# An attention and MLP kernel: left rows in quarters of the array, left values inside the last block, left queries with the second half, and a written-out order

## The chip, the cores and the metric

The kernel runs on one core of a Trainium2 chip. A core has five engines that work side by side and each take their instructions in order: PE (the matrix engine, with PEld for its weight loads), DVE (VectorE), ACT (ScalarE), POOL (GpSimd) and SP (SyncE, which here only issues DMA transfers). The metric is device time in microseconds (us) of one execution, as the median of several runs; lower is better.

## The reference

Four batches of eight heads, 576 positions, head size 64. Rotary attention is followed by an MLP with a piecewise activation:

```python
scores = scale * np.matmul(q_rot, k_rot.transpose(0, 1, 3, 2))
scores = scores - np.max(scores, axis=-1, keepdims=True)
attn = np.exp(scores)
attn = attn / (np.sum(attn, axis=-1, keepdims=True) + 1e-09)
attn_out = np.matmul(attn, v)
x = attn_out.transpose(0, 2, 1, 3).reshape(B * S, H * D)      # 2304 x 512
h = x @ w_in                                                  # 512 x 2048
g = np.where(h >= 1, h, np.where(h <= -1, 0.0, (h + 1) ** 2 / 4.0))
return g @ w_out                                              # 2048 x 512
```

The data is drawn so large that one fp16 value is not enough. Every operand of a product is therefore kept as a sum of two fp16 numbers, and each product is three products (`TERMS`: high by high, high by low, low by high).

## The kernel before, in words

**Rows.** A batch has 576 query rows: four tiles of 128 (the main rows) and 64 left rows. Work goes in eight blocks, two for each batch: tiles 0 and 1, then tiles 2 and 3 (the batch's last block). The heads go in four pairs `j`.

**Scores and softmax.** One item is a tile and a pair of heads (`scores`, L582): 12 matmuls, in which the two heads use the upper and the lower 64 rows of the array and write `psS[0]` and `psS[1]`; three products of 512 columns and three of 64 columns for each head. The softmax of an item (`softmax_item`) is, for each head, a maximum on DVE (`mx`, L556), an exponential on ACT (L558), the high half of the normalised row on ACT (L566) and its low half on DVE (`phl`, L568). SP then issues a transposing DMA from `phl` into `pT` (L300).

**Values.** For a block and a pair of heads `pv_group` runs 28 matmuls (L611), 14 for each head, of 256 columns, the two heads side by side in the left and the right 64 columns of the array. After two pairs `x_out` moves 512 columns of `psV` to `xT` (ACT L626, DVE L629).

**The left rows** have a path of their own, after the last block of each batch (`attention_left`). `prep_left` loads, turns and splits their queries into `qL`, a tile with the two heads of a pair on the diagonal and zeros elsewhere. For each pair one full-width group of six matmuls (`scores_left`, L594) gives 64 rows of both heads in one tile `psS[z]`, a softmax over one such tile follows, one transposing DMA of half the size, and 28 matmuls of 64 columns (`pv_left`, L611). One `x_out` of 256 columns for each batch writes `xL`.

**The MLP** takes each block in 8 steps. A step is two groups of 12 matmuls of 256 columns into `psH` (L692), the activation (ACT L699, L711; DVE L702, L709, L713, the last of which writes the low half of `g`), and two groups of six matmuls of 512 columns into `psO` (L722). The left rows of two batches together make one more MLP of 4 steps with groups of 128 columns. So there are 72 steps in all.

**The weights** come as 64-bit floats. `prep_w` turns each of 16 chunks into two fp16 halves: three passes on DVE (L506, L508, L510) over a staging buffer, then work on ACT and on PE (L535, L536) or DVE (L527).

**The order.** Every step is entered into a `Plan` with its engine, an estimated cost and the keys it reads and writes. `Plan.order()` simulates the engines with these costs, takes at each point the step with the lowest rank, where the rank is a due time plus the numbers of the table `SLACK`, and returns one list. The steps are written into the program in the order of this list, so it sets the queue of each engine.

## Time and profile before

| | |
|---|---|
| median of 3 runs | 636.88 us |
| lowest and highest run | 633.86 and 639.57 us |
| span of the profiled execution, first to last instruction | 632.0 us |
| PE, DVE and ACT busy in that span | 559.8, 511.2 and 441.0 us |

The profile is of one execution. Its span leaves out what lies around the instructions, and of that execution only the span is known; it stands 4.88 us under the median of the runs. Busy times come from this one execution; durations of instructions that follow each other closely overlap a little, so that a chain of start times is a better measure of a group than the sum of its instructions.

### The profile page before, as it was taken

The page shows a single profiled execution, that of the slowest core. Times are in us where ns is not written, and L with a number is a line of the kernel's source. Part 1 is how long each engine was busy: PE and PEld are TensorE (multiplying, and loading weights), DVE is VectorE, ACT ScalarE, POOL GpSimd, SP SyncE. Part 2 cuts the span into 40 slices and gives each one's busy share as a digit, 9 for nine tenths or more (in the row PEclk, how much of TensorE's full clock was granted, in tenths as well). Part 3 has the DMA queues.
Part 4 walks back from the last instruction along what each step waited for, and adds up shares of the span by engine and source line. Part 5 has one row for each costly group of instructions (what it writes and reads, how often), then busy time and mean ns, then how long its engine had stood idle before and what let it go on. Part 6 is the DMA issues. An engine that isn't in the chain of part 4 may idle for free.

```text
span 632.0 us, 12652 instructions
## 1 busy us (share of the span) xinstructions
PE 559.8 (89%) x5078; PEld 358.6 (57%) x5078; DVE 511.2 (81%) x839; ACT 441.0 (70%) x881; POOL 7.5 (1%) x18
## 2 busy tenths in 40 slices
PE   1346678799997999999998999999999999999995
PEld 1112234566654666666665676676666676666663
DVE  5998999999999999998897889889877874333422
ACT  3647898978999799984878798877787663232221
POOL 0000100000000000000000000000000000000000
PEclk9997879999998999999999999999999999999999
DMA  8997988695699858876377765856666553000000
GB/s 265 372 305 261 258 231 161 133 233 132 142 260 203 195 99 188 205 164 161 92 163 129 124 127 109 136 94 115 113 131 129 85 99 77 1 8 27 1 34 18
DMA packets 188011, 91.33 MB, mean 145 GB/s; under 512 B 170160, under 2 KB 178608, under 8 KB 185904
## 3 DMA queue, kind: packets, MB, share of 16 engines
q1 hardware_dynamic: 186224, 77.94, 56.0%
q0 software_dynamic: 1728, 12.58, 5.6%
q8 instruction: 40, 0.66, 0.4%
q14 instruction: 19, 0.16, 0.1%
HBM read 40.96 MB, written 4.72 MB: 72 GB/s over the span
## 4 chain that ended last, share of the span: by engine, by line
PE 56%; DVE 22%; DMA 12%; ACT 6%; issue 3%; SPq 0%; ACTq 0%
PE psO L722 21%; PE psH L692 21%; PE psV L611 7%; PE psS L582 5%; DMA pT<-phl 5%; DVE phl L568 4%; DVE mx L556 3%; DMA rk<-in_km_dram 3%; DMA vM<-vS 2%; ACT p L558 2%; DVE g L713 1%; ACT phl L566 1%; DMA rv<-in_vm_dram 1%; DVE r L709 1%; DVE xT L508 1%
## 5 line engine op out<-in xcount | busy, mean ns | idle before, releaser
L722 PE MATMUL psO<-w,g 128*128 128x512 f16 x864 | 211.7, 380 | 1.9 <-ACT g L711 0.9
L692 PEld LDWEIGHTS <-w 128*128 128x128 f16 x1920 | 170.9, 98 | 44.4 <-issue 5.2
L692 PE MATMUL psH<-xT,w 128*128 128x256 f16 x1536 | 187.7, 273 | 3.2 <-ACT a L699 3.2
L558 ACT ACTIVATE p<-psS,mx 128x576 f32<-128x576 f32 x144 | 105.3, 733 | 26.1 <-DVE mx L556 20.1
L722 PEld LDWEIGHTS <-g 128*128 128x128 f16 x864 | 79.3, 98 | 75.2 <-DVE g L713 2.5
L568 DVE SCALAR_TENSOR_TENSOR phl<-p,sums,phl 128x576 f16<-128x576 f32 x144 | 113.4, 812 | 9.6 <-ACT phl L566 9.6
L566 ACT ACTIVATE phl<-p,sums 128x576 f16<-128x576 f32 x144 | 105.0, 765 | 17.5 <-DVE sums L563 15.2
L556 DVE TENSOR_REDUCE mx<-psS 128x1 f32<-128x576 f32 x144 | 104.3, 750 | 6.9 <-PE psS L582 6.2
L582 PE MATMUL psS<-kT,qT 64*128 64x512 f16 (+1 forms) x768 | 64.5, 295 | 22.6 <-ACT p L558 15.3
L711 ACT ACTIVATE g<-r 128x512 f16<-128x512 f32 x72 | 44.9, 624 | 47.5 <-DVE r L709 29.2
L699 ACT ACTIVATE a<-psH 128x512 f32<-128x512 f32 x72 | 42.4, 590 | 49.3 <-PE psH L692 48.7
L713 DVE SCALAR_TENSOR_TENSOR g<-r,g 128x512 f16<-128x512 f32 x72 | 49.5, 688 | 26.8 <-ACT g L711 26.7
L582 PEld LDWEIGHTS <-qT 64*128 64x128 f16 x768 | 31.2, 97 | 68.5 <-issue 47.9
L702 DVE SCALAR_TENSOR_TENSOR r<-a 128x512 f32<-128x512 f32 x48 | 33.1, 689 | 45.6 <-ACT a L699 45.2
L611 PE MATMUL psV<-pT,vS 128*64 128x256 f16 (+1 forms) x768 | 50.1, 253 | 3.8 <-DMA pT<-phl 3.5
L709 DVE SCALAR_TENSOR_TENSOR r<-a,r 128x512 f32<-128x512 f32 x72 | 49.6, 689 | 0.9
L611 PEld LDWEIGHTS <-vS 128*64 128x64 f16 x768 | 33.3, 112 | 18.5 <-issue 14.7
L611 PE MATMUL psV<-pT,vM 128*64 128x256 f16 (+1 forms) x480 | 29.2, 253 | 3.3 <-DMA vM<-vS 3.3
L558 ACT ACTIVATION_READ_ACCUMULATOR p<-psS,mx 128x1 f32 x144 | 28.1, 195 | 0.0
L692 PE MATMUL psH<-xL,w 128*128 128x128 f16 x384 | 25.5, 219 | 0.0
L611 PEld LDWEIGHTS <-vM 128*64 128x64 f16 x480 | 22.0, 113 | 4.1 <-DMA vM<-vS 3.8
L535 PE MATMUL psO<-xT,xL 128*128 128x512 f32 x20 | 15.4, 864 | 9.8 <-DVE xT L510 5.6
(98 smaller groups left out, 467.5 us busy)
## 6 DMA issues: line engine op xcount, KB each, us to landing
w<-in_w_in_dram POOLq DMA_DIRECT2D x5, 1024.0 KB, 6.9
rv<-in_vm_dram SPq DMA_DIRECT2D x8, 512.0 KB, 5.7
w<-in_w_out_dram POOLq DMA_DIRECT2D x4, 1024.0 KB, 7.3
out_dram<-o SPq DMA_DIRECT2D x16, 256.0 KB, 2.4
rq<-in_qm_dram SPq DMA_DIRECT2D x7, 512.0 KB, 7.2
dup<-in_qm_dram SPq DMA_DIRECT2D x7, 512.0 KB, 3.9
dup<-in_km_dram SPq DMA_DIRECT2D x6, 576.0 KB, 5.3
rk<-in_km_dram SPq DMA_DIRECT2D x6, 576.0 KB, 6.8
```

Of the source, the lines that this page charges most:

```text
L556: plan.add("dve", dve_cost(S, psum=True), at, lambda m=m, src=src: nc.vector.tensor_reduce(out=m, in_=src, op=ALU.max, axis=AX.X, negate=T ...
L558: plan.add("act", act_cost(S, psum=True, ptrs=2), at, lambda a=a, e=e, m=m, src=src: nc.scalar.activation(out=p32[e], in_=src, func=AF.Exp ...
L566: plan.add("act", act_cost(S), at, lambda a=a, e=e, hi=hi: nc.scalar.activation(out=hi, in_=p32[e], func=AF.Copy, scale=rr[:, a:a + 1]), r ...
L568: plan.add("dve", dve_cost(S, ptrs=1), at, lambda a=a, e=e, hi=hi, lo=lo: nc.vector.scalar_tensor_tensor(out=lo, in0=p32[e], scalar=rr[:, ...
L582: nc.tensor.matmul(out=psS[a][:, lo:hi], lhsT=qT[hf][d, l, j, c:c + 128], rhs=kT[ks][d, j, m, lo:hi], start=z == 0, stop=z == 2)
L611: nc.tensor.matmul(out=outs[a], lhsT=st, rhs=moving(a, blk), start=z == 0, stop=z == len(seq) - 1)
L692: nc.tensor.matmul(out=psH[:, n * i:n * i + n], lhsT=wi[ft // 2][:, wl, kk, 128 * (ft % 2):128 * (ft % 2) + 128], rhs=xfn(xl, kk), start=z ...
L699: plan.add("act", act_cost(512, psum=True, ptrs=0), at, lambda one=one: nc.scalar.activation(out=a, in_=psH, func=AF.Relu, scale=2.0 ** -7 ...
L709: plan.add("dve", dve_cost(512), at, lambda one=one: nc.vector.scalar_tensor_tensor(out=r, in0=a, scalar=one, in1=r, op0=ALU.max, op1=ALU. ...
L711: plan.add("act", act_cost(512, ptrs=0), at, lambda g=g, one=one: nc.scalar.activation(out=g[:, 0], in_=r, func=AF.Relu, scale=1.0, bias=- ...
L713: plan.add("dve", dve_cost(512), at, lambda g=g, one=one: nc.vector.scalar_tensor_tensor(out=g[:, 1], in0=r, scalar=-one, in1=g[:, 0], op0 ...
L722: nc.tensor.matmul(out=psO[pos[tt]], lhsT=g[:, gl, n * i + 128 * tt:n * i + 128 * tt + 128], rhs=wo[ft // 2][:, wl, ft % 2, :], start=ft = ...
```

## The change

1. **Left scores.** `scores_left` now takes two pairs of heads at a time. Each of the four heads uses one quarter of the array: 64 rows by 64 columns. The heads of the first pair write the two halves of `psS[0]`, those of the second pair `psS[1]`, in the order `psS[0]`, `psS[1]`, `psS[0]`, `psS[1]`, and a group has 24 matmuls. It takes the place of two groups of six. The softmax after it is an ordinary one over two tiles, and four smaller transposing DMAs (64 rows each) take the place of two of 128 rows.
2. **Left values.** The left rows of a head lie in `pT` beside the 256 main rows of the last block, and the 28 value matmuls of that block now have 320 columns. `pv_left` is gone. In the last block `x_out` runs after each pair, over 320 columns, and writes main and left rows into one `xT[1]`; `xL` is gone, and the left MLP reads two pieces of 64 columns from `xT[1]`.
3. **Left queries** are loaded, turned and split with the second half of the queries, which now has 320 columns instead of 256. `prep_left`, `rqL` and `qL` with its zeros are gone.
4. **Small tiles** (`mx`, `sums`, `ones` and others) are columns of `sca`; the identity for the weights lies in `xT[1]`. For odd `j` the two heads of an item change places in `psS`.
5. **The order** is a written list. `ORDER` holds, for each place, the index of the next step among those still left; costs, `mode` and `late` of a step are recorded and not read.

```diff
-SLACK = {
-    "k0.03 dve": -18_500, "k1 act": 68_700, "k1 dve": 128_000, "k1.12 dve": 2_700, "k1.20 dve": 192_800,
...
+ORDER = """
+1 1 2 10 0 1 4 3 22 0 14 14 18 38 93 31 110 31 49 35 68 69 68 53 129 48 228 119 226 5 2 4 16 4 2 4 3 2 4 0 3 0 6
...
     def order(self):
-        steps, users = self.steps, self.users()
...
-        return [steps[i][3] for i in out]
+        left = list(range(len(self.steps)))
+        return [self.steps[left.pop(int(k))][3] for k in ORDER.split()]
...
-    qT = [sbt(f"qT{i}", [128, 2, NP, 256], F16) for i in range(2)]
-    qL = [sbt(f"qL{i}", [128, 2, NP, 128], F16) for i in range(2)]
+    qT = [sbt(f"qT{i}", [128, 2, NP, QW[i]], F16) for i in range(2)]
...
-    pT = [sbt(f"pT{i}", [128, 18, 256], F16) for i in range(2)]
-    xT = [sbt(f"xT{i}", [128, 2, KT, 256], F16) for i in range(2)]
-    xL = sbt("xL", [128, 2, KT, 128], F16)
+    pT = [sbt(f"pT{i}", [128, 18, 320], F16) for i in range(2)]
+    xT = [sbt(f"xT{i}", [128, 2, KT, 256 + 128 * i], F16) for i in range(2)]
...
-        n = len(js)
+        n, m, src = len(js), QW[hf], (qa, qb)[hf]
         x = rq[i][:, js[0]:js[0] + n, :]
...
-        dma(at, x, qm[0, b][:, js[0]:js[0] + n, 256 * hf:256 * hf + 256], [], xk, 128 * 4 * n * 256)
-        dma(at, y, qm[1, b][:, js[0]:js[0] + n, 256 * hf:256 * hf + 256], [], yk, 128 * 4 * n * 256)
...
         plan.group = f"q{min(b, 1)}"
-        turn(at, x, xk, y, yk, 256 * hf, 256, n)
+        turn(at, x, xk, y, yk, 256 * hf, m, n)
...
-    def prep_left(b, at):
-
-        plan.part = b
-        plan.group = f"raw q{min(b, 1)}"
-        dma(at, rqL, ql[b], [], ["rqL0", "rqL1"], 128 * 2048)
-        plan.group = f"ql{min(b, 1)}"
-        s = b % 2
-        turn(at, rqL[:, 0], ["rqL0"], rqL[:, 1], ["rqL1"], SM, SL, NP)
-        by = [(j, j + 1) for j in range(NP)] if b == 0 else [(0, NP)]
-        for a in range(2):
-            c = slice(64 * a, 64 * a + 64)
-            for j0, j1 in by:
-                split(at, qL[s][c, 0, j0:j1, c], [("qL", s, 0, a, j) for j in range(j0, j1)],
-                      qL[s][c, 1, j0:j1, c], [("qL", s, 1, a, j) for j in range(j0, j1)],
-                      rqL[c, 0, j0:j1, :], ["rqL0"], qfac[b, j0], 64 * (j1 - j0), 64 * a, 64)
...
             for lo, hi in ((0, SM), (SM, S)):
                 for z, (l, m) in enumerate(TERMS):
                     for a in range(2):
-                        d = slice(64 * a, 64 * a + 64)
+                        h = a ^ (j & 1)
+                        d = slice(64 * h, 64 * h + 64)
                         nc.tensor.matmul(out=psS[a][:, lo:hi], lhsT=qT[hf][d, l, j, c:c + 128],
                                          rhs=kT[ks][d, j, m, lo:hi], start=z == 0, stop=z == 2)
...
-        plan.add("pe", 760.0, at, mm, r=[("qT", hf, j, x) for x in range(2)] + [("kT", ks, j, x) for x in range(2)],
-                 w=[("psS", 0), ("psS", 1)])
-
-    def scores_left(at, b, j):
-        ks, z = b % 2, j % 2
+        plan.add("pe", 748.0, at, mm, r=[("qT", hf, j, x) for x in range(2)] + [("kT", ks, j, x) for x in range(2)],
+                 w=[("psS", 0), ("psS", 1)], mode="rows", late=[([("kT", ks, j, 1)], 213.0), ([("qT", hf, j, 1)], 427.0)])
+
+    def scores_left(at, b, j0):
+
+        ks = b % 2
 
         def mm():
             for lo, hi in ((0, SM), (SM, S)):
-                for i, (l, m) in enumerate(TERMS):
-                    nc.tensor.matmul(out=psS[z][:, lo:hi], lhsT=qL[ks][:, l, j, :], rhs=kT[ks][:, j, m, lo:hi],
-                                     start=i == 0, stop=i == 2)
-
-        plan.add("pe", 760.0, at, mm, r=[("qL", ks, l, a, j) for l in range(2) for a in range(2)] + ["qL0"]
-                 + [("kT", ks, j, x) for x in range(2)], w=[("psS", z)])
-        return z
+                for z, (l, m) in enumerate(TERMS):
...
+                    for h in range(2):
+                        d = slice(64 * h, 64 * h + 64)
+                        for e in range(2):
+                            o = 64 * (h ^ e)
+                            nc.tensor.matmul(out=psS[e][o:o + 64, lo:hi], lhsT=qT[1][d, l, j0 + e, 256:256 + SL],
+                                             rhs=kT[ks][d, j0 + e, m, lo:hi], start=z == 0, stop=z == 2)
+
+        js = (j0, j0 + 1)
+        plan.add("pe", 850.0, at, mm, r=[(x, i, j, l) for x, i in (("qT", 1), ("kT", ks)) for j in js for l in range(2)],
+                 w=[("psS", 0), ("psS", 1)], mode="quad",
+                 late=[([("kT", ks, j, 1) for j in js], 213.0), ([("qT", 1, j, 1) for j in js], 427.0)])
...
     def pv_group(at, j, slot, n, c0, pkeys):
-        plan.add("pe", pe_cost(14, n + 58) + 130, at, lambda: values(
-            [psV[64 * a:64 * a + 64, c0:c0 + n] for a in range(2)], lambda a, i: pT[slot][:, 9 * a + i, 0:n], j),
-            r=vkeys + pkeys, w=["psV"])
-
-    def pv_left(at, j, slot, pkeys):
-        plan.add("pe", pe_cost(14, 122), at, lambda: values(
-            [psV[64 * a:64 * a + 64, 64 * j:64 * j + 64] for a in range(2)],
-            lambda a, i: pT[slot][:, i, 64 * a:64 * a + 64], j), r=vkeys + pkeys, w=["psV"])
+        plan.add("pe", pe_cost(14, n + 5), at, lambda: values(
+            [psV[64 * a:64 * a + 64, c0:c0 + n] for a in range(2)],
+            lambda a, i: pT[slot][:, 9 * (a ^ (j & 1)) + i, 0:n], j),
+            r=vkeys + pkeys, w=["psV"], mode="cols")
...
-    def attention_block(b, ts, at):
-
-        n = 128 * len(ts)
+            out=dst[1], in0=src if len(dst[0].shape) == 2 else src.rearrange("p (k n) -> p k n", k=2),
+            scalar=f, in1=dst[0], op0=ALU.mult, op1=ALU.subtract), r=["psV", fk] + keys[0], w=keys[1])
+
+    def attention_block(b, ts, at, last):
+
+
...
-        per = 512 // n
+        assert xs == last
+        e = b % 2
+        c0 = SL * (last and e == 0)
+        cl = 0 if e == 0 else 256
+        n = 256 + SL * last
         for j in range(NP):
-            slot = ring("pT", 2)
+            if j % 2 == 0:
+                slots = [ring("pT", 2) for _ in range(2)]
+            slot = slots[j % 2]
             for i, t in enumerate(ts):
+                if last and j % 2 == 0 and i == 1:
+                    plan.group, plan.part = f"left{min(b, 1)}", f"{b}{j}"
+                    scores_left(at - 0.5, b, j)
+                    s = softmax_item(at - 0.5, 2)
+                    for z in range(2):
+                        for h in range(2):
+                            dmaT(at - 0.5, pT[slots[z]][:, 9 * h:9 * h + 9, cl:cl + SL], phl[s][64 * h:64 * h + 64, 2 * S * z:2 * S * z + 2 * S],
+                                 [("phl", s, l, z) for l in range(2)], [("pT", slots[z], 2 + h)], 64 * 2304)
...
-                dmaT(at, pT[slot][:, :, 128 * i:128 * i + 128], phl[s],
+                dmaT(at, pT[slot][:, :, c0 + 128 * i:c0 + 128 * i + 128], phl[s],
                      [("phl", s, l, a) for l in range(2) for a in range(2)], [("pT", slot, i)], 128 * 4608)
...
             plan.group, plan.part = f"pv{min(b, 1)}", f"{b}{ts[0]}{j}"
-            pv_group(at - 1, j, slot, n, n * (j % per), [("pT", slot, i) for i in range(len(ts))])
-            if j % per == per - 1:
-                g = j // per
-                if n == 256:
-                    dst = [xT[xs][:, l, 2 * g:2 * g + 2, :].rearrange("p k n -> p (k n)") for l in range(2)]
-                else:
-                    dst = [xT[xs][:, l, :, 0:128] for l in range(2)]
-                x_out(at - 1, b, dst, [("xT", xs, l, g) for l in range(2)], 512)
-        xk = [("xT", xs, l, g) for l in range(2) for g in range(4 // per)]
-        return (lambda l, kk: xT[xs][:, l, kk, 0:n]), xk, n
-
-    def attention_left(b, at):
-        for j in range(NP):
-            slot = ring("pT", 2)
-            plan.group, plan.part = f"left{min(b, 1)}", f"{b}{j}"
-            z = scores_left(at, b, j)
-            s = softmax_item(at, 1, z)
-            dmaT(at, pT[slot][:, 0:9, 0:128], phl[s][:, 0:2 * S],
-                 [("phl", s, l, 0) for l in range(2)], [("pT", slot, 0)], 128 * 2304)
-            pv_left(at, j, slot, [("pT", slot, 0)])
-            at += 0.5
-        e = b % 2
-        x_out(at, b, [xL[:, l, :, 64 * e:64 * e + 64] for l in range(2)], [("xL", l, e) for l in range(2)], 256)
+            if last:
+                pv_group(at - 1, j, slot, n, 0, [("pT", slot, i) for i in range(4)])
+                x = SL * e
+                x_out(at - 1, b, [xT[1][:, l, j, x:x + n] for l in range(2)],
+                      [[("xT", 1, l, j), ("xL", l, e, j)] + (["idn", ("ndg", 0), ("ndg", 1)] if b == 0 else []) for l in range(2)], n)
+                continue
+            pv_group(at - 1, j, slot, n, n * (j % 2), [("pT", slot, i) for i in range(len(ts))])
+            if j % 2:
+                x_out(at - 1, b, [xT[0][:, l, j - 1:j + 1, :] for l in range(2)], [[("xT", 0, l, i) for i in (j - 1, j)] for l in range(2)], 512)
+        xk = [("xT", xs, l, j) for l in range(2) for j in range(NP)]
+        return (lambda l, kk: xT[xs][:, l, kk, SL * last:SL * last + 256]), xk, 256
 
...
-        for x in qL:
-            nc.vector.memset(x, 0.0)
...
-            mlp_block(lambda l, kk: xL[:, l, kk, :], [("xL", l, e) for l in range(2) for e in range(2)], 128,
+            mlp_block(lambda l, kk: xT[1][:, l, kk, :].rearrange("p (g n) -> p g n", n=SL)[:, 0:6:5, :],
+                      [("xL", l, e, j) for l in range(2) for e in range(2) for j in range(NP)], 128,
                       [done + span * (m + nst + 0.5) for m in range(4)], left_rows(b - 1))
```

DVE around the low half of `g` of the 16th MLP step (`g_84` before, `g_81` now). Before:

```order
L709 SCALAR_TENSOR_TENSOR r<-a,r 128x512
L563 RECIPROCAL sums_109<-sums_109 128x2
L316 TENSOR_REDUCE sca<-psV 128x1
L713 SCALAR_TENSOR_TENSOR g_84<-r,g_84 128x512
L318 TENSOR_SCALAR sca<-sca 128x1
L568 SCALAR_TENSOR_TENSOR phl_75<-p_0_71,sums_109,phl_75 128x576
```

Now:

```order
L478 SCALAR_TENSOR_TENSOR phl_73<-p_0_69,sca,phl_73 128x576
L466 TENSOR_REDUCE sca<-psS_93 128x1
L625 SCALAR_TENSOR_TENSOR r<-a,r 128x512
L270 TENSOR_TENSOR rq_85<-rq_85,dup_88 128x1024
L473 RECIPROCAL sca<-sca 128x2
L629 SCALAR_TENSOR_TENSOR g_81<-r,g_81 128x512
L466 TENSOR_REDUCE sca<-psS_93 128x1
```

The write of `g` moves from row 367 of DVE's queue to row 362.

DVE early in the program, where the first weight chunk is turned (`xT_79` and `xT_77` are its staging buffer, `mx` or `sca<-psS` the first maximum). Before:

```order
L556 TENSOR_REDUCE mx_0_100<-psS_112 128x1
L556 TENSOR_REDUCE mx_1_101<-psS_113 128x1
...
L345 TENSOR_TENSOR rk<-rk,w 128x576
L354 SCALAR_TENSOR_TENSOR kT_62<-rk,sca,kT_62 128x576
L354 SCALAR_TENSOR_TENSOR qT_64<-rq_88,sca,qT_64 128x256
...
L506 TENSOR_SCALAR xT_79<-w 128x1024
L506 TENSOR_SCALAR o<-w 128x1024
L508 SCALAR_TENSOR_TENSOR xT_79<-w,xT_79 128x1024
```

Now:

```order
L270 TENSOR_TENSOR rk<-rk,w 128x576
L416 TENSOR_SCALAR xT_77<-w 128x1024
L243 TENSOR_SCALAR sca<-sca 128x1
L466 TENSOR_REDUCE sca<-psS_92 128x1
L466 TENSOR_REDUCE sca<-psS_93 128x1
L246 RECIPROCAL sca<-sca 128x1
L418 SCALAR_TENSOR_TENSOR xT_77<-w,xT_77 128x1024
```

The first weight pass moves from behind the fourth split of the keys to ahead of the first maximum.

SP at the first left rows of batch 0 (`128x18x128` is the transposing DMA of an item, the smaller ones are those of left rows). Before:

```order
L300 DMA_TRANSPOSE pT_77<-phl_75 128x18x128
L300 DMA_TRANSPOSE pT_76<-phl_74 128x9x128
L296 DMA rv<-in_vm_dram 128x1024 x2
L300 DMA_TRANSPOSE pT_77<-phl_75 128x9x128
L300 DMA_TRANSPOSE pT_76<-phl_74 128x9x128
L296 DMA dup_90<-in_qm_dram 128x4x256
```

Now:

```order
L225 DMA_TRANSPOSE pT_74<-phl_72 128x18x128
L225 DMA_TRANSPOSE pT_74<-phl_73 128x9x64 x2
L225 DMA_TRANSPOSE pT_75<-phl_73 128x9x64 x2
L221 DMA rvL<-in_vl_dram 64x512
L221 DMA rq_85<-in_qa_dram 128x1024
L221 DMA dup_88<-in_qa_dram 128x1024
```

Four half-height transposes stand in a row, in the middle of the last block instead of behind it.

## Rows read from the trace of the kernel before

**Rows 1.** The page: span, busy time, and busy tenths in 40 equal slices.

```profile
span 632.0 us, 12652 instructions
...
PE 559.8 (89%) x5078; PEld 358.6 (57%) x5078; DVE 511.2 (81%) x839; ACT 441.0 (70%) x881; POOL 7.5 (1%) x18
...
PE   1346678799997999999998999999999999999995
...
DVE  5998999999999999998897889889877874333422
```

**Rows 2.** Stretches: length, busy PE, PEld, DVE, ACT, POOL, granted clock, DMA.

```profile
0.00:120.00 120.00, 65.13 (x389) 33.21 (x390) 108.12 (x201) 85.31 (x169) 5.41 (x14) 0.93 0.86 250
120.00:242.50 122.50, 114.94 (x1075) 73.71 (x1074) 119.86 (x184) 108.20 (x216) 2.10 (x4) 0.97 0.80 182
242.50:340.00 97.50, 94.27 (x885) 61.35 (x884) 89.91 (x140) 79.13 (x160) 0.00 (x0) 1.00 0.70 159
340.00:620.00 280.00, 280.00 (x2710) 188.16 (x2707) 191.23 (x315) 166.41 (x335) 0.00 (x0) 1.00 0.44 83
```

**Rows 3.** Chain that ended last, around 500 us: start, us, engine, tile, line.

```profile
502.45 0.73 PE psS L594 x6
...
514.50 1.65 PE psV L611 x28
...
520.63 1.29 PE psO L722 x6
521.93 0.56 PE psV L611 x28
522.49 1.40 PE psO L722 x6
```

**Rows 4.** The same chain near 238 us.

```profile
237.96 0.84 PE psS L582 x12
```

**Rows 5.** DVE groups by line and shape: count, busy us, mean ns, idle before.

```profile
L568 DVE SCALAR_TENSOR_TENSOR phl<-p,sums,phl 128x576 f16<-128x576 f32 x144 | 113.4, 812 | 9.6 <-ACT phl L566 9.6
...
L556 DVE TENSOR_REDUCE mx<-psS 128x1 f32<-128x576 f32 x144 | 104.3, 750 | 6.9 <-PE psS L582 6.2 <-PE psS L594 0.6
...
L629 DVE SCALAR_TENSOR_TENSOR xT<-psV,sca,xT 128x512 f16<-128x512 f32 x16 | 11.9, 746 | 2.5 <-ACT xT L626 2.3
...
L345 DVE TENSOR_TENSOR rq<-rq,dup 128x1024 f32<-128x1024 f32 x7 | 8.6, 1222 | 0.0
...
L354 DVE SCALAR_TENSOR_TENSOR qL<-rqL,sca,qL 64x256 f16<-64x256 f32 x6 | 2.8, 472 | 0.1
...
L354 DVE SCALAR_TENSOR_TENSOR qL<-rqL,sca,qL 64x64 f16<-64x64 f32 x8 | 2.2, 280 | 0.1
L629 DVE SCALAR_TENSOR_TENSOR xL<-psV,sca,xL 128x256 f16<-128x256 f32 x4 | 1.9, 478 | 0.2 <-ACT xL L626 0.2
L341 DVE TENSOR_TENSOR rqL<-rqL,rt 128x256 f32<-128x256 f32 x4 | 1.7, 420 | 1.5 <-DMA rqL<-in_ql_dram 1.5
...
L345 DVE TENSOR_TENSOR rq<-rq,w 128x256 f32<-128x256 f32 x4 | 1.7, 416 | 0.0
...
L754 DVE MEMSET qL<- 128x512 uint32 x2 | 1.0, 485 | 0.2 <-issue 0.2
```

**Rows 6.** DVE in order of time: the low halves of `g` of steps 16 and 24.

```profile
241.80 0.69 DVE L713 SCALAR_TENSOR_TENSOR g<-r,g 128x512 f16<-128x512 f32 x1
...
299.50 0.68 DVE L713 SCALAR_TENSOR_TENSOR g<-r,g 128x512 f16<-128x512 f32 x1
```

**Rows 7.** Tile `pT`: its transposing DMAs on SP (ns, shortest, median, longest), and their landing.

```profile
L300 SPq DMA_TRANSPOSE pT<-phl x80: 1242/2690/7948, 28.6 to 524.5; - x80
...
DMA to landing us min/median/max: 3.2/4.6/10.2
```

**Rows 8.** The end of the chain that ended last.

```profile
624.15 2.35 PE psO L722 x10
...
626.52 0.69 ACT o L732
```

More of the change, by code (lines that the diff above doesn't have):

```diff
@@ L87, in __init__, with add, dep @@
         self.part = ""
-    def add(self, eng, cost, at, fn, r=(), w=(), bw=0.0, turn=False):
+    def add(self, eng, cost, at, fn, r=(), w=(), bw=0.0, turn=False, mode="full", late=()):
         i = len(self.steps)
-        deps = set()
+        deps = {}
+        after = {k: ns for keys, ns in late for k in keys}
+        def dep(d, k):
+            if d != i:
+                deps[d] = min(deps.get(d, 1e9), after.get(k, 0.0))
         for k in r:
             if k in self.writer:
-                deps.add(self.writer[k])
+                dep(self.writer[k], k)
             self.readers.setdefault(k, []).append(i)
```

210 lines of the change are left out of this document (44 added, 166 removed), and 55 rows, old and new, of the table ORDER.

## The prediction

> **What bounds the kernel now.** I read the page first, then sums over stretches, then the chain that ended last, then the groups of DVE. The slices of the page show PE nearly full from about the sixth slice to the end, and DVE full from the second slice to about the twentieth [rows 1]. The stretches put numbers on it [rows 2]. Up to 120 us PE is busy for 65.1 us while DVE is busy for 108.1 of 120. From 120 to 242.5 DVE still has 119.9 of 122.5, and PE waits 7.6 us. From 242.5 to 340 PE waits 3.2 us, and from 340 to 620 it waits for nothing: 280.00 of 280. ACT is never as full as DVE in these rows. So the end is set by two queues in a row: DVE's queue up to some place in the first 340 us, and from that place PE's whole remaining queue. Something taken from PE counts if it stands behind that place; something taken from DVE counts if it stands ahead of it. After the last matmul come one eviction and the output [rows 8], the same in both kernels.
>
> **Left values.** A left value group of 28 matmuls takes 0.56 us on PE from its start to the next group's, and the group ahead of it is 0.11 us longer than usual, 1.40 against 1.29 [rows 3]. This goes 16 times: 16 x 0.67 = 10.7 us. In exchange the 16 value groups of the last blocks get 64 more columns. A main group of 256 columns takes 1.65 and a left one of 64 takes 0.56, so a column of all 28 costs (1.65 - 0.56) / 192 = 5.7 ns and 64 columns 0.36 us; 16 x 0.36 = 5.8 us come back. Net -4.9 us.
>
> **Left scores.** A full-width group takes 0.73 us [rows 3]; 16 of them are 11.7 us. In their place come 8 groups in quarters, of which the trace of before has none. The lower bound is that the quarters run side by side, like the two halves of a main item do: 0.84 us [rows 4], plus 0.11 for the change of layout ahead of it, 0.95. The upper bound is that only two quarters run at a time: twice 0.73, plus 0.11 at either end, 1.68. I take 1.07: a main item, plus the change, plus six more short matmuls at the 0.02 us each that 28 short ones show in 0.56. The nearest row is the main item, since there too different parts of the array write different tiles. 8 x 1.07 = 8.6, net -3.1 us; the bounds give -4.1 to +1.7. Both edits together take 8.0 us from PE.
>
> [Rows 4] has two row halves of the array at work on two separate tiles; no row shows two row halves writing into one tile at once, which the two quarters of `psS[0]` would do. The Trainium skill, page "TensorEngine Tiling (Array Packing)", section "Restrictions and Gotchas", speaks against it: "Different row tiles cannot access same PSUM bank simultaneously." By that rule the quarters of one tile would take turns, which is the first rival below; by the row they would not.
>
> **Left queries, on DVE.** Gone are 12 turning passes of 0.42, six splits of 0.47 and eight of 0.28, and two fills of 0.49 us [rows 5]: 5.0 + 5.1 + 1.0 = 11.1 us. The 12 turning passes over second halves get 256 more columns; from 1222 ns for 1024 and 416 for 256 columns [rows 5] a column costs 1.05 ns and 256 columns 0.27 us, 3.2 us in all, and their splits 1.1 us. The moves out of `psV` were 8 of 746 and 4 of 478 ns in the last blocks [rows 5]; now they are 16 of 320 columns, 0.545 by the same slope, 0.8 us more. Net -6.0 us on DVE over the whole program. ACT loses about as much and is not full. The four fewer query loads are off the path.
>
> **The new order, at two places.** Every engine's queue is rewritten, so I count, at a given MLP step, what stands ahead of it on DVE and behind it on PE, in both queues. Step 16 is the last step of batch 0's last block; before, DVE ends its `g` at 242.5 [rows 6]. Behind its first `psO` group PE has in both kernels the same 37 main items, 94 and 32 `psH` groups and 228 runs of three `psO` matmuls. What differs is the change's own: 12 value groups longer by 0.36 (+4.3), 12 left value groups gone (-8.0), 12 left score groups gone (-8.8), five quarter groups come (+5.4): -7.1 us. Ahead of it DVE has nine turning passes of `rqL` less (-3.8), ten splits of `qL` less (8 x 0.28 + 2 x 0.47 = -3.2), no fills (-1.0), two low halves of `phl` at 0.81 more (+1.6), 6 turning passes of 1024 and 6 of 1280 columns instead of 11 of 1024 (+2.8), longer splits (+0.5), and moves out of `psV` (+0.2): -2.9 us. Together 10.0 us earlier.
>
> Step 24, whose `g` ended at 300.2 [rows 6], is the second place. Behind it PE has four main items fewer (-3.4), 8 value groups longer (+2.9), no left value groups (-8.0) and four quarter groups for nine left score groups (-2.3): -10.8. Ahead of it DVE has 14 turning passes of 1024 and two of the keys less and nine of 1280 more (-6.4), nothing of `qL` (-10.1), 7 maxima and 6 low halves more (+10.2), the rest about even (+0.1): -6.2. Together 17.0 us earlier. So places behind step 16 gain more than step 16 does; the new order evens out the front and is not better there than what the change itself removes.
>
> **The sum.** Against the profiled execution: step 16 and all behind it come 10.0 us sooner. The 3.2 us that PE still waits between 242.5 and 340 [rows 2] belong to places like step 24 that come earlier by more, so I let 2.0 of them go: 632.0 - 10.0 - 2.0 = 620.0 us of span. The median of the runs stood 4.88 us over the span; with the same distance 624.9, and I say 625 us. About 1% is what a measurement of this kernel can tell from no change, since its three runs spread over 0.9%.
>
> **Moved waits that I cost at nothing.** SP gets four half-height transposes where it had two; the value groups that read them wait behind other PE work, and in the new order some 20 us at the least of PE groups stand between each quarter group and the first value group that needs it. In the last blocks a value group now waits for the move of the pair before it out of `psV`, some 1.3 us of ACT and DVE; other PE groups stand between them. If a cover is gone, the wait is what the DMA's landing takes, 4.6 us [rows 7], or that 1.3 us.
>
> **Rivals.**
> - *The quarters take turns.* A quarter group then costs 1.68, five of them stand behind step 16: 5 x 0.61 = 3.1 us back, 628 us. For it: no row has this layout. Against: both halves of the array, by rows and by columns, do run side by side in the rows.
> - *The front gets shorter as well.* DVE is idle for 11.9 us in the first 120 [rows 2], and the new order fills early gaps with the first weight pass. If 5 us of these go and all of the 3.2, 10.0 + 5 + 3.2 = 18.2 us go: 619 us.
> - *The front gets longer.* The same early pass needs its raw weights sooner, and SP now loads them ahead of the third and fourth keys. If DVE's idle time in the first 120 us grows from 11.9 to 20, 8 us of the 12 are lost: 633 us, no change that can be told.
> - *SP's queue makes the values late, and the kernel slower.* An ordinary left transpose takes SP at least 1.24 us and an item's 2.69 [rows 7]. If a half-height one takes as long as a whole, each of the 8 quarter groups keeps SP 2.5 us longer, and the loads and transposes queued behind it, with the value groups that wait for them, are late by as much: 8 x 2.5 = 20 us against 12, 645 us. It decides from 1.5 us exposed for each group. For it: SP takes its queue in order, and transposes were waited for before. Against it: the cover on PE named above.
>
> **How the numbers follow.** The forecast has 0.50, the shorter front 0.17, quarters in turns 0.10, the longer front 0.15, SP's queue 0.08. The first three are faster by over 1% (below 630.5), less a little for the upper part of the forecast's own spread: 0.74 faster, 0.18 within 1%, 0.08 slower. The range reaches from 614, below the shorter front, to 634, just over the longer front; it leaves out the slower case and a little on either side.
>
> **What would show it.** Quarter groups of 1.0 to 1.1 us from start to start (1.6 or more: they take turns); value groups of 320 columns at 2.0; DVE's total near 505 us; the `g` of step 16 about 3 us earlier, near 239.6 (well over 243: the longer front); no PE wait worth naming after it, and PE full to the end. The prediction is wrong if DVE's idle time in the first 120 us differs much from 11.9, if PE waits at the start of value groups for transposes, or if PE has waits behind 340 that before did not have.

## The result, and the profile after

By its ratio the changed kernel is faster: 0.9753, 95% interval 0.9719 to 0.9786, on a median before of 636.14 us now measured over 20 runs; that is some 620.4 us where 625 was forecast. This ratio and those below take of each kernel only the runs within 1.5% of its quickest, here 5 of the changed kernel's 20. By the median of all its 20 runs, 635.25 us, nothing is gained: its executions differ more than those of before, 617.19 to 656.04 us against 631.96 to 639.57, and the experiments on the front below ask why.

The page of the changed kernel, lines that answer to [rows 1]: span, busy time, busy tenths.

```profile
span 619.4 us, 11916 instructions
...
PE 551.4 (89%) x4726; PEld 352.7 (57%) x4726; DVE 503.7 (81%) x807; ACT 433.5 (70%) x863; POOL 7.2 (1%) x18
...
PE   2447679769799999999999989999999999999996
...
DVE  6979979989899999898999877979886877534341
```

PE lost 8.4 us of work and DVE 7.5; 8.0 and 6.0 were forecast. The same stretches as in [rows 2]:

```profile
0.00:120.00 120.00, 71.36 (x425) 36.44 (x426) 105.41 (x190) 84.43 (x164) 5.06 (x14) 0.91 0.96 238
120.00:242.50 122.50, 110.74 (x982) 71.12 (x980) 118.79 (x175) 107.68 (x215) 2.10 (x4) 1.00 0.83 195
242.50:340.00 97.50, 96.75 (x862) 63.40 (x864) 90.95 (x145) 83.62 (x172) 0.00 (x0) 1.00 0.77 152
340.00:619.40 279.40, 272.60 (x2466) 181.76 (x2466) 188.51 (x300) 157.74 (x315) 0.00 (x0) 1.00 0.44 86
```

DVE is idle for 14.6 us of the first 120, where it was 11.9. PE waits 0.8 us between 242.5 and 340. The chain of waits around 500 us shows the new groups, as [rows 3] and [rows 4] did the old ones:

```profile
468.14 0.86 PE psS L510 x24
469.01 3.18 PE psV L528 x56
472.18 0.84 PE psS L493 x12
...
502.02 0.86 PE psS L510 x24
502.89 2.02 PE psV L528 x28
504.91 1.42 PE psH L607 x12
...
607.41 7.14 PE psO L638 x33
614.54 0.02 issue
614.57 0.69 ACT o L649
```

L510 is a quarter group: 0.86 to 0.87 us, hardly more than the main item of 0.84 behind it, and 2.02 us is a value group of 320 columns. Its last two lines answer to [rows 8]: PE ends at 614.5, 12.0 us sooner than before.

To read the sum I cut both traces where DVE ends the low half of `g` of step 16 [rows 6]; in the changed kernel that is

```profile
241.34 0.69 DVE L629 SCALAR_TENSOR_TENSOR g<-r,g 128x512 f16<-128x512 f32 x1
```

at 242.0, against 242.5. The stretches ahead of it and behind it up to PE's end, columns as in [rows 2]; first the kernel before, then the changed one:

```profile
0.00:242.50 242.50, 180.07 (x1462) 106.93 (x1463) 227.98 (x384) 193.52 (x384) 7.51 (x18) 0.95 0.83 216
242.50:626.50 384.00, 379.72 (x3619) 251.71 (x3616) 283.22 (x457) 246.76 (x497) 0.00 (x0) 1.00 0.50 101
```

```profile
0.00:242.00 242.00, 181.59 (x1401) 107.33 (x1402) 223.70 (x364) 191.62 (x376) 7.16 (x18) 0.96 0.89 217
242.00:614.50 372.50, 369.81 (x3326) 245.40 (x3324) 279.96 (x445) 241.18 (x487) 0.00 (x0) 1.00 0.53 104
```

Behind the cut PE has 9.9 us less work and waits 2.7 us instead of 4.3. Ahead of it DVE has 4.3 us less work, but is idle for 18.3 us instead of 14.5. So the 12.0 us come almost wholly from behind the cut, and most of what DVE saved ahead of it is given back in waits. The longest of these are for the high halves that ACT writes, and ACT waits for transposes (its row stands with the experiments):

```profile
DVE phl L478 <- ACT phl L476: 8.6, 7, 2.7
```

Such a row gives the total of a wait in us, how often it came, and the longest. The tile `pT` between 57 and 150 us shows where; SP's transposes (ns, shortest, median, longest) and their landing, as in [rows 7]:

```profile
L225 SPq DMA_TRANSPOSE pT<-phl x16: 1201/3458/9352, 57.2 to 149.6; - x16
...
DMA to landing us min/median/max: 2.7/6.3/15.1
```

Before, the longest one of this stretch kept SP 6.9 us and the slowest landing took 10.2; now it is 9.4 and 15.1, though six of the 16 are half-height ones, which take as little as 1.20.

### The profile page after: what moved, and what is told of

Read it like the earlier page. It is cut to its first block, busy times and chain, and to the rows that moved or that the text cites. A ratio compares the mean times of both kernels' runs of the same rounds, so it can differ in the third digit from the quotient of the medians.

```text
span 619.4 us, 11916 instructions
## 1 busy us (share of the span) xinstructions
PE 551.4 (89%) x4726; PEld 352.7 (57%) x4726; DVE 503.7 (81%) x807; ACT 433.5 (70%) x863; POOL 7.2 (1%) x18
## 4 chain that ended last, share of the span: by engine, by line
PE 65%; DVE 14%; DMA 12%; ACT 5%; issue 2%; SPq 1%; ACTq 0%; DVEq 0%
PE psO L638 25%; PE psH L607 25%; DMA pT<-phl 9%; PE psV L528 7%; PE psS L493 6%; DVE phl L478 3%; DVE sca L466 2%; ACT p L468 2%; DMA vM<-vS 1%; ACT phl L476 1%; PE psS L510 1%; PE psO L445 1%; DVE rk L270 1%; DMA rq<-in_qa_dram 1%; DVE w L437 1%
## 5 line engine op out<-in xcount | busy, mean ns | idle before, releaser
L607 PE MATMUL psH<-xT,w 128*128 128x256 f16 (+1 forms) x1920 | 205.8, 262 | 4.7 <-ACT a L615 4.7
L638 PE MATMUL psO<-w,g 128*128 128x512 f16 x864 | 203.2, 379 | 2.4 <-DVE g L629 1.5
L468 ACT ACTIVATE p<-psS,sca 128x576 f32<-128x576 f32 x144 | 105.5, 735 | 34.6 <-DVE sca L466 17.4
L478 DVE SCALAR_TENSOR_TENSOR phl<-p,sca,phl 128x576 f16<-128x576 f32 x144 | 115.4, 813 | 16.5 <-ACT phl L476 16.2
L476 ACT ACTIVATE phl<-p,sca 128x576 f16<-128x576 f32 x144 | 107.9, 767 | 29.3 <-DMA pT<-phl 15.4
L466 DVE TENSOR_REDUCE sca<-psS 128x1 f32<-128x576 f32 x144 | 105.4, 751 | 7.4 <-PE psS L493 5.9
L629 DVE SCALAR_TENSOR_TENSOR g<-r,g 128x512 f16<-128x512 f32 x72 | 49.5, 687 | 31.4 <-ACT g L627 31.2
L528 PE MATMUL psV<-pT,vS 128*64 128x256 f16 (+1 forms) x512 | 43.3, 292 | 3.4 <-DVE xT L542 2.5
L468 ACT ACTIVATION_READ_ACCUMULATOR p<-psS,sca 128x1 f32 x144 | 28.2, 196 | 0.0
L473 DVE RECIPROCAL sca<-sca 128x2 f32<-128x2 f32 x72 | 11.6, 161 | 14.9 <-ACT sca L471 14.8
L236 PE MATMUL psV<-sca 128*128 128x3 f32 (+2 forms) x26 | 6.0, 299 | 16.8 <-ACT w L230 9.4
## 6 DMA issues: line engine op xcount, KB each, us to landing
w<-in_w_in_dram POOLq DMA_DIRECT2D x5, 1024.0 KB, 10.7
w<-in_w_out_dram POOLq DMA_DIRECT2D x4, 1024.0 KB, 10.7
```

Of the source, the lines that this page charges most:

```text
L466: plan.add("dve", dve_cost(S, psum=True), at, lambda m=m, src=src: nc.vector.tensor_reduce(out=m, in_=src, op=ALU.max, axis=AX.X, negate=T ...
L468: plan.add("act", act_cost(S, psum=True, ptrs=2), at, lambda a=a, e=e, m=m, src=src: nc.scalar.activation(out=p32[e], in_=src, func=AF.Exp ...
L476: plan.add("act", act_cost(S), at, lambda a=a, e=e, hi=hi: nc.scalar.activation(out=hi, in_=p32[e], func=AF.Copy, scale=rr[:, a:a + 1]), r ...
L478: plan.add("dve", dve_cost(S, ptrs=1), at, lambda a=a, e=e, hi=hi, lo=lo: nc.vector.scalar_tensor_tensor(out=lo, in0=p32[e], scalar=rr[:, ...
L528: nc.tensor.matmul(out=outs[a], lhsT=st, rhs=moving(a, blk), start=z == 0, stop=z == len(seq) - 1)
L607: nc.tensor.matmul(out=psH[:, n * i:n * i + n], lhsT=wi[ft // 2][:, wl, kk, 128 * (ft % 2):128 * (ft % 2) + 128], rhs=xfn(xl, kk), start=z ...
```

## The experiments

Three kernels take the structure apart, one gives the old planner the new structure, and eight ask what lengthens the front. Unless a diff says otherwise, each is the changed kernel with its order.

**Full-width left scores.**

```diff
-                            nc.tensor.matmul(out=psS[e][o:o + 64, lo:hi], lhsT=qT[1][d, l, j0 + e, 256:256 + SL],
-                                             rhs=kT[ks][d, j0 + e, m, lo:hi], start=z == 0, stop=z == 2)
+                        nc.tensor.matmul(out=psS[e][:, lo:hi], lhsT=qT[1][:, l, j0 + e, 192:192 + 2 * SL],
+                                         rhs=kT[ks][:, j0 + e, m, lo:hi], start=z == 0, stop=z == 2)
```

> Each left-score group of 24 quarter matmuls is replaced by two full-width groups of six, as before the change (on the tile's left and last main rows together, so heads are mixed and the values are not the reference's); order, softmax and everything else stay. Theory A (from the place near 174 us on, PE's queue sets the end, so the changed kernel gains what its PE groups save): a left-score step goes from 0.87 to about 1.46 us plus at most 0.1, six of the eight lie behind that place, so 3.5 to 4.5 us longer than the changed kernel, some 623 to 624 us of span against 619.4. Theory B (the order brought the gain, the left groups were covered): no longer than 1 us more.

Measured: ratio to before 1.0115 (1.006 to 1.0171). The cut at step 16 separates two things:

```profile
0.00:259.80 259.80, 187.14 (x1364) 110.31 (x1364) 224.16 (x363) 191.54 (x376) 7.19 (x18) 0.91 0.88 202
259.80:635.50 375.70, 373.37 (x3273) 247.19 (x3266) 280.31 (x445) 242.20 (x487) 0.00 (x0) 1.00 0.53 103
```

Behind the cut PE has 3.6 us more work for five steps of 1.47 to 1.56 us in place of 0.87, and that part is 3.2 us longer: theory A's price for each group, of which five and not six lie behind this cut. The steps are the safer measure, since one and the same queue took 372.1 to 374.9 us there in the executions below. Ahead of the cut DVE's work is the same (224.16), but its waits rose from 18.3 to 35.6 us, which the edit doesn't touch. So the whole time tells nothing of the edit, and from here on I compare stretches; the front became a question of its own.

**Split values.**

```diff
+        cuts = ((0, n),) if n == 256 else ((c1, c1 + 256), (cl, cl + SL))
...
-        plan.add("pe", pe_cost(14, n + 5), at, lambda: values(
-            [psV[64 * a:64 * a + 64, c0:c0 + n] for a in range(2)],
-            lambda a, i: pT[slot][:, 9 * (a ^ (j & 1)) + i, 0:n], j),
+            for x, y in cuts:
+                values([psV[64 * a:64 * a + 64, c0 + x:c0 + y] for a in range(2)],
+                       lambda a, i: pT[slot][:, 9 * (a ^ (j & 1)) + i, x:y], j)
```

> The value groups of the last blocks run as 28 matmuls of 256 columns and then 28 of 64 columns, adjacent, in place of 28 of 320; nothing else changes. Theory A: 1.65 + 0.56 in place of 2.02 us, 0.19 us each, 16 of them, of which at least 12 lie behind the binding place: 2.3 to 3.0 us longer than the changed kernel; as the left groups stand next to the main ones no change of layout is added, so this is less than the 4.9 us of the prediction's term. Theory B (values are covered by other work): under 1 us.

Measured: ratio 1.0031 (0.9988 to 1.0074). A step of both groups takes 2.09 us in the chain of waits, and behind the cut at 253.8 PE has 370.56 us of work against 369.81 (a difference too small to tell by itself):

```profile
263.29 2.09 PE psV L528 x56
```

```profile
0.00:253.80 253.80, 186.42 (x1514) 111.42 (x1514) 224.30 (x364) 191.83 (x376) 7.19 (x18) 0.93 0.90 207
253.80:626.80 373.00, 370.56 (x3662) 251.68 (x3660) 279.91 (x445) 241.67 (x487) 0.00 (x0) 1.00 0.52 104
```

My 0.19 us a group was wrong; it is 0.07. The 1.65 and 0.56 us of groups that stand alone [rows 3] each seem to hold one more change of layout at their end. So of the 0.30 us that merging saves for each group (1.65 + 0.56 + 0.11 - 2.02), 0.07 is the second run of 28 matmuls and 0.23 the changes of layout. Two main value groups in a row agree: 3.18 us, 0.12 less than twice 1.65.

**Separate tiles for the row halves.**

```diff
-                            nc.tensor.matmul(out=psS[e][o:o + 64, lo:hi], lhsT=qT[1][d, l, j0 + e, 256:256 + SL],
+                            nc.tensor.matmul(out=psS[h][o:o + 64, lo:hi], lhsT=qT[1][d, l, j0 + e, 256:256 + SL],
...
-                                 [("phl", s, l, z) for l in range(2)], [("pT", slots[z], 2 + h)], 64 * 2304)
+                                 [("phl", s, l, z ^ h) for l in range(2)], [("pT", slots[z], 2 + h)], 64 * 2304)
```

> In the left-score groups the quarters of the upper row half write psS[0] and those of the lower row half psS[1], so that two row halves no longer write one tile at the same time; the transposes take their rows from the other tile accordingly. If two row halves in one tile cost nothing (theory A): 0.87 us for a group as in the changed kernel, to within 0.02. If they hinder each other: less than 0.84 us.

Measured: one run of 676.94 us, no ratio. DVE waits 57.7 us ahead of step 16 in it, so its long time is the front's again. From its chain of waits, the last two of eight groups:

```profile
513.41 0.86 PE psS L525 x24
557.74 0.86 PE psS L525 x24
```

No difference: two row halves that write one tile, into different partitions, don't hinder each other here.

**The old planner.** `Plan`, `SLACK` and `RAMP` of the kernel before order the changed kernel's steps.

```diff
-        left = list(range(len(self.steps)))
-        return [self.steps[left.pop(int(k))][3] for k in ORDER.split()]
+        rank = [x + SLACK.get(s[5], 0.0) + SLACK.get(s[8], 0.0) for x, s in zip(self.wanted(), steps)]
...
+        return [steps[i][3] for i in out]
```

> All of the change's structure, but the order comes from the planner and the slack table of the kernel before, which were made for the old steps. Theory A (the gain is what left the PE and DVE queues): PE busy stays near 551 us and DVE near 504; the time lies between the changed kernel and before, some 622 to 632 us. Theory B (the new order brought it): 636 us or more, the structure alone gains nothing.

Measured: ratio 1.0401 (1.0369 to 1.0433), 658.63 to 662.02 us.

```profile
0.00:267.40 267.40, 189.51 (x1400) 111.07 (x1402) 236.19 (x373) 197.67 (x384) 7.19 (x18) 0.92 0.77 205
267.40:651.60 384.20, 375.92 (x3328) 244.62 (x3324) 271.57 (x435) 241.54 (x480) 0.00 (x0) 0.99 0.48 95
```

The tile `pT` in this run from 57 to 150 us:

```profile
L298 SPq DMA_TRANSPOSE pT<-phl x14: 1220/2736/7682, 61.4 to 138.7; - x14
...
DMA to landing us min/median/max: 2.8/4.8/9.8
```

Theory A's range fell: the structure without a fitting order is slower than before. This list puts 12.5 us more DVE work ahead of step 16, DVE waits 31.2 us there, and PE waits 8.3 us behind it. So the written order is part of the gain; next to a table of slack made for other steps, it keeps later work off DVE in the front. The two lines of `pT` matter below: in this order the same transposes, beside the same loads, are about as quick as before.

**The front.** Six kernels change SP's queue or a buffer there. Where a diff has `r`, the list of SP's steps is permuted and every other engine's queue is that of `ORDER`.

Loads of raw weights behind those of queries:

```diff
+        r[20:28] = [r[i] for i in (21, 22, 24, 26, 20, 23, 25, 27)]
```

> Only SP's queue changes: the third and fourth load of raw weights are issued after the loads of the fourth keys, the second half of the queries and the fourth query pair. In the changed kernel DVE stood idle 2.7 us before the turning of those queries and 1.1 us before the fourth pair's, at 33 to 39 us. Theory A (DVE's queue in the front reaches the end): these 3.8 us go, and 1 to 4 us of the time with them. Rival (the transposes between 57 and 135 us, which take SP 4.8 us each there against 2.7 elsewhere, set the front): DVE's early idle time goes but comes back as waits of ACT and DVE for transposes by 135 us, time within 1 us of the changed kernel.

Measured: median 644.05 us of four runs, 629.44 to 646.7, no ratio. The first half of theory A holds; in the first 40 us DVE has 34.42 us of work done instead of 30.76:

```profile
0.00:40.00 40.00, 13.30 (x65) 7.33 (x66) 34.42 (x92) 24.70 (x53) 1.90 (x8) 1.00 0.99 347
```

and the rival holds for the rest: the `g` of step 16 ends at 263.4. ACT waits for transposes to free its buffers.

Moves of value halves (`vM`) behind the fourth transpose, alone and with the edit above:

```diff
+        r[32:36] = [r[i] for i in (35, 32, 33, 34)]
```

> Changed kernel, with one thing moved in SP's queue: the three moves of value halves between partitions (vM) that stood ahead of the fourth transpose now stand behind it. In the changed kernel that transpose, issued at 57.2 us right behind the moves, took SP 5.77 us and landed after 15 us, and the next two took 5.56 and 7.77; undisturbed ones take 2.7; in the two experiments before, the two that followed took 7.5 and 12.3, and 16.2 and 11.6. Theory C (transposes that share the DMA engines with these moves are slow, and ACT, DVE and PE wait for the buffers that they free): the fourth to sixth transpose take 2.7 to 4 us each, the waits of ACT for transposes between 40 and 180 us fall from 11.5 us (25 and 31 us in the two experiments) to under 8, the span is 612 to 618 us. Rival D (the loads of raw weights that GpSimd issues slow them): nothing changes there, the same transposes still take 5 to 16 us.

> As the run with the moves behind the transpose, and the third and fourth load of raw weights also behind those of the queries, which gave DVE 3.7 us more of work in the first 40 us. Theory C: both add up, the early 3.7 us now reach the end, 608 to 616 us of span. Rival D: the early gain is lost again to waits for transposes between 60 and 150 us, 619 us or more.

Measured: 0.9907 (0.987 to 0.9944) and 0.9878 (0.9826 to 0.9929); the medians of all runs are 636.38 us of 14 and 642.56 of six, the lowest 624.83 and 625.08. The tile `pT` from 50 to 89 us, first in the changed kernel, then with the moves behind, and below that, for the latter, what PE waited for from 40 to 180 us:

```profile
L225 SPq DMA_TRANSPOSE pT<-phl x5: 3643/5560/7770, 48.5 to 85.1; - x5
...
DMA to landing us min/median/max: 11.3/13.1/15.1
```

```profile
L241 SPq DMA_TRANSPOSE pT<-phl x4: 2415/3025/4645, 48.5 to 84.2; - x4
...
DMA to landing us min/median/max: 4.6/5.8/9.4
```

```profile
PE psV L544 <- DMA pT<-phl: 10.5, 1, 10.5
PE psV L544 <- DMA vM<-vS: 7.5, 1, 7.5
```

Theory C's transposes, the fourth to the sixth, came out as forecast, 2.4 to 3.0 us, but the span did not (640.5 us in the profiled execution, where 612 to 618 was forecast): PE's values now wait for the moves and for one transpose, and the transposes issued at 89 and 96 us, at times of loads of raw weights, take 6.5 and 7.9 us instead.

The changed kernel again, beside these:

> The changed kernel once more, beside the other runs of this call. Theory C and rival D alike: 617 to 656 us; where it is long, ACT's waits for transposes between 40 and 180 us are long by as much, and the stretch from 240 us on is the same as before to within 1 us.

Measured: 633.39 to 655.7 us in six runs, median 648.94, no ratio. Its profile, of an execution of 648.2 us, agrees: ACT's waits for transposes in the front are long, while the cut at step 16 leaves 374.8 us behind it, as everywhere.

```profile
ACT phl L476 <- DMA pT<-phl: 32.4, 4, 14.2
```

In the changed kernel's first profile the same row was

```profile
ACT phl L476 <- DMA pT<-phl: 11.5, 6, 3.2
```

This run stood on one chip with the two edits of the moves. There both were quicker than the changed kernel, by the medians as by the lowest runs, so theory C's edit may have brought some 10 us; with runs that spread this far, six of them don't settle it.

Two of three loads that GpSimd issues at 120 us moved to SP, at 107 and 115 us:

```diff
-        dma(at, raw, (w_out if which else w_in).bitcast(U32)[c], [], rk_, 128 * 8192, "sp" if i < 4 else "pool", [] if i < 4 else ["poolq"])
+        dma(at, raw, (w_out if which else w_in).bitcast(U32)[c], [], rk_, 128 * 8192, "sp" if i < 4 or i in (13, 14) else "pool", [] if i < 4 or i in (13, 14) else ["poolq"])
...
+        r[44:44] = late[:1]
+        r[47:47] = late[1:]
```

> Changed kernel with two loads of raw weights (of the three that GpSimd issues within 1 us at 120 us) issued by SP instead, one after the transpose at 107 us and one after that at 115 us, where the DMA engines were 0.40 busy. Theory E (the transpose at 126.7 us, 9.35 us on SP in the changed kernel and 10.8 to 18 in the runs after it, is slow because 3 MB of weights load beside it): that transpose takes 2.7 to 5 us, ACT's wait for it (3.2 us in the changed kernel, 8 and more in the others) falls below 1 us, 3 to 10 us sooner than a changed kernel that runs alike up to 120 us. Theory C (the moves between partitions at 53 to 56 us make transposes slow): no help there, the transposes at 57 to 85 us stay at 5 to 16 us.

Measured: 0.9893 (0.983 to 0.9955), median of all 12 runs 639.18. A miss: the transpose that theory E wanted at 2.7 to 5 us, now issued at 129.7, took SP 11.1 us, and ACT waits for it 5.7 us. The row holds it and the next one:

```profile
129.69 14.56 SPq L244 DMA_TRANSPOSE pT<-phl  x2
```

Four buffers for the first eight items, two of them in the second key tile:

```diff
+    phl += [kt1[:, 4 * S * i:4 * S * i + 4 * S] for i in range(2)]
...
-        s, ri = ring("phl", 2), ring("sums", 4)
+        s, ri = e % 4 if e < 8 else ring("phl", 2), ring("sums", 4)
```

> Changed kernel, but the first eight items use four buffers for the normalised rows in turn, the two extra ones in the second key tile, which is not in use until some 120 us; order unchanged. If ACT and DVE wait in the front only for these buffers to be read by slow transposes: ACT's waits for transposes between 40 and 100 us (8.4 us in the changed kernel, 18 to 27 in others) fall below 2 us, the transposes stay slow, and the time is 5 to 15 us below that of the changed kernel on the same chip. If the values' wait for pT is what binds: ACT's waits move to PE, no gain.

Measured: 1.0107 (1.0038 to 1.0175), median of all six runs 646.91. SP's queue from 57 us on, and below it what PE waited for longest from 40 to 180 us:

```profile
57.20 5.71 SPq L227 DMA_TRANSPOSE pT<-kT  x1
66.56 12.81 SPq L227 DMA_TRANSPOSE pT<-phl  x1
...
87.88 19.36 SPq L227 DMA_TRANSPOSE pT<-phl  x1
```

```profile
PE psV L531 <- DMA pT<-phl: 19.2, 1, 19.2
```

The buffers are not the cause: with more of them the transposes are as slow, and the wait goes to PE's values. Later, with two buffers again, ACT waits 17.1 us for one transpose, and DVE 12.6 us for a load of raw weights.

Both of these and the earlier loads together:

> Both of these, and the third and fourth load of raw weights behind those of the queries (3.7 us more of DVE work in the first 40 us). If the front is DVE's queue plus waits for transposes, all three add up: last wait of PE above 0.8 us before 170 us, span 605 to 614 us. If something else in the front binds: 619 us or more.

Measured: 1.0 (0.9965 to 1.0036), a span of 632.8 us where 605 to 614 was forecast. PE's values wait 11.9 us for one transpose. Nothing adds up.

**Loads left out.** Eleven of GpSimd's twelve loads of raw weights bring 32 columns of 2048.

```diff
-        dma(at, raw, (w_out if which else w_in).bitcast(U32)[c], [], rk_, 128 * 8192, "sp" if i < 4 else "pool", [] if i < 4 else ["poolq"])
+        n = 2048 if i < 4 or i == 14 else 32
+        dma(at, raw[:, 0:n], (w_out if which else w_in).bitcast(U32)[c][:, 0:n], [], rk_, 128 * 8192, "sp" if i < 4 else "pool", [] if i < 4 else ["poolq"])
```

> Changed kernel in which eleven of the twelve loads of raw weights that GpSimd issues bring 16 KB instead of 1 MB (the rest of those weights is left at what lies in the buffer, so the output is not the reference's); every instruction of PE, DVE, ACT and SP stays in its place. Rival D (these loads make the transposes between 57 and 150 us slow): all transposes there take 2.7 to 4 us but the one right behind the moves between partitions, ACT's waits for transposes between 40 and 180 us fall below 5 us, span 600 to 615 us, and repeated runs lie within 1.5% of each other. Theory C (the moves alone make them slow): the transposes at 57 to 77 us still take 5 to 16 us, the waits stay above 10 us, 617 us or more.

Measured: 0.965 (0.9617 to 0.9683), 609.45 to 614.37 us in six runs. The cut at step 16:

```profile
0.00:231.30 231.30, 180.42 (x1402) 107.53 (x1402) 223.39 (x364) 191.14 (x376) 7.25 (x18) 0.96 0.73 177
231.30:604.90 373.60, 371.40 (x3326) 246.61 (x3324) 279.67 (x444) 241.30 (x487) 0.00 (x0) 1.00 0.52 103
```

The tile `pT` from 57 to 150 us:

```profile
L225 SPq DMA_TRANSPOSE pT<-phl x16: 1201/2671/4770, 63.7 to 147.4; - x16
...
DMA to landing us min/median/max: 2.7/4.6/10.1
```

Rival D holds: without the loads no transpose takes SP longer than 4.77 us, and the one right behind the moves, here issued at 54.0, takes 2.69. DVE's work ahead of the cut is the same to 0.3 us, its waits fall from 18.3 to 7.9, the `g` of step 16 comes 10.7 us sooner, and PE ends 9.6 us sooner, at 604.9. What the front gives reaches the end. Most of it is the way over ACT, whose row with DVE was 8.6 above:

```profile
DVE phl L479 <- ACT phl L477: 0.8, 1, 0.8
```

Some 3 us are not: DVE's waits for loads of queries fall as well, from 3.8 us to 0.7. The six runs lie within 0.8% of each other, so the spread is gone too. Nor is it the clock: the mean clock granted to PE ahead of the cut is 0.96 of the higher level in both kernels. Theory C alone falls: moves and transposes without the loads don't disturb each other.

## Why the prediction was right, step by step

The bound was the right one. In every kernel here with the changed kernel's order, but the one with separate tiles, whose PE waits 12 us behind the cut, the part behind step 16 takes 372 to 376 us and DVE's work ahead of it 223 to 225; the ends from 604.9 to 650.7 us differ by DVE's waits ahead of step 16, 7.9 to 51.8 us. That is the forecast's picture of two queues in a row. PE's granted clock behind the cut is 1.00 in all of these, the higher of its two levels (2.4 GHz), so it doesn't tell them apart there.

| term, us | forecast | measured |
|---|---|---|
| PE's work behind step 16 | -7.1 | -9.9 |
| PE's waits behind it | -2.0 | -1.6 |
| DVE's work ahead of it | -2.9 | -4.3 |
| DVE's waits ahead of it | 0 | +3.8 |
| PE's end | -12.0 | -12.0 |

The sum is right, but three of its terms are off and nearly cancel: 2.8 and 1.4 us more came off PE's and DVE's work than forecast, and 3.8 went back in DVE's waits.

**What was luck.** That the sum agrees to a tenth is chance: in its second profile the changed kernel took 374.8 us behind the cut and not 372.5, and PE's work there went from 369.7 to 371.5 us in nine executions of the same groups, so single terms are known to no better than some 2 us. And it is the sum of a quick execution. 13 of the 20 runs took over 632 us, nearer to the 633 of the rival of the longer front, which had a chance of 0.15, or beyond it. The forecast is right for executions whose front is not held up, and nothing in it foresaw how few those would be. Two of its signs of being wrong came in part: DVE's idle time in the first 120 us is 14.6, and behind 340 PE waits 1.9 us for an exponential of ACT, where before it had no wait up to 620. The `g` of step 16 ended at 242.0, and not near 239.6.

**PE.** The value group of 320 columns is 2.02 as forecast. The quarter group is 0.87, not 1.07, and even below the bound of 0.95: the change of layout that I added to it is not there as a term of its own. Five groups behind the cut make 1.0 us of the 2.8. Some 0.5 comes from the four places there where the new order puts two value groups next to each other (0.12 each). The last 1.3 us I can't assign, and that is less than what one queue's executions differ by. The weight of left values in the sum (-4.9) was right, but what it consists of is mostly changes of layout, as the split showed. One row was misread, without harm to the sum: in [rows 3] the group that is 0.11 us longer stands behind the value group, not ahead of it (0.56 at 521.93, then 1.40 at 522.49). The Trainium skill, page "TensorEngine Tiling (Array Packing)", section "Key Properties", says that changing the tiling mode drains TensorE; the trace fits this, with 0.12 us at the end of a run of value groups and 0.11 in the group behind it.

**The quarters don't take turns.** The rule that I weighed, from the same page's "Restrictions and Gotchas", would have made them 1.68. By the trace, 0.87 in one tile and 0.86 in two, it doesn't hold in this form for two quarters that lie in different partitions of one tile.

**DVE in the front** is the step that failed. I let its idle time stay, with the row of the first 120 us (11.9), and priced a longer front at a delay of loads. Loads did delay DVE less than before (3.8 us ahead of the cut against 9.4), but the transposes became slow, which I had costed at nothing on the ground that PE groups cover them. They are covered for the values; what I missed is that ACT needs the transposed buffer back, and that DVE and PE queue behind ACT. The rival of SP's queue had the right place and the wrong price: half-height transposes take 1.20 us, about half of a whole one's 2.67, and it is the whole ones that grew. DVE's work itself was right: its instructions ahead of the cut add up to 257.0 us before and 254.1 now, the 2.9 of the forecast; busy time, 4.3 less, counts overlaps once.

**From span to time.** I carried over the 4.88 us between the span and the median of before. The profiled execution of the changed kernel took 621.23 us for a span of 619.4, a distance of 1.83. If before's was the same, its profiled execution took 633.8, some 2.3 us under its median. Hence 625 where some 620.4 was measured; the span itself came out at 619.4 for 620.0.

**What made transposes slow** is shown in part. It takes the loads of raw weights: without them they are quick. The loads suffer as well: their page row for `w_in` has a median landing of 10.7 us where before had 6.9. It takes this order's front too, since the old planner's order, with the same steps and loads, has them at a median of 2.7. Putting the moves elsewhere made three of them quick and others slow. The Trainium skill, page "DMA: Bandwidth & Descriptors", section "Queues, rings and completion order", says that a DMA engine goes round its queues a packet at a time; that would fit SP's queue of small packets (0.43 KB in the mean of the page) beside GpSimd's of large ones (7.3 KB), but no run here shows the mechanism, nor why one execution of the same kernel suffers more than another. An order with the loads where SP has no transpose was not found. The lowest run of a full computation is the changed kernel's, 617.19 us; that none of the tries beats it is not shown, since on the one chip where they ran side by side two of them were quicker.

## What to carry to other kernels

Cut the trace at the place from which one queue sets the end, and compare work and waits on either side of it: a change to one side is then measured to 2 or 3 us, and a single group to hundredths, even where whole runs differ by thirty. Look at the spread of all runs before a ratio of the quickest. Cost a step on a packed array with the changes of layout on both of its sides, and put steps of one layout next to each other. When work moves into an early part that is full of loads, ask for every DMA there who waits for its buffer to come back, not only who reads what it brings.

## What the runs showed of the hardware

- Four quarters of the array, two to a tile, run nearly as fast as two halves: 0.87 us for 24 matmuls against 0.84 for 12.
- A value group of 1.65 us that stands alone is 0.12 us longer than one with another behind it: 3.18 for two in a row, 2.09 for 256 and 64 columns, 2.02 for 320.
- A transpose of 2.67 us, undisturbed, kept SP for up to 20.6 us (19.4 and 20.6 in the run with four buffers) beside loads of 1 MB that another engine had issued.
